# Fourier mixing and a hard-swish MLP on one core: the inverse transform's last stage as even and odd sums of mirrored tokens

## The chip, the cores and the metric

The kernel runs on one core of one Trainium2 chip. The metric is device microseconds of the whole program on that core; a verdict compares medians of several runs on the same chip. The core's engines are named as in the profile: PE (TensorE, with PEld for its weight loads), DVE (VectorE), ACT (ScalarE), POOL (GpSimd) and SP (SyncE, which here only issues DMAs).

## The reference

All data are 32-bit floats. `x` has 8 batches of 3008 tokens with 256 features.

```python
X = np.fft.rfft(x, axis=1)
Y = X * (filt_r + 1j * filt_i)[None, :, :]
y = np.fft.irfft(Y, n=3008, axis=1)
t = y.reshape(8 * 3008, 256)
h = t @ w_in                           # 256 -> 2048
g = h * np.clip(h + 3.0, 0.0, 6.0) / 6.0
out = g @ w_out                        # 2048 -> 256
```

## The kernel before

**The transform.** 3008 tokens are 47 times 64. A batch goes through four stages, each a set of small matrix products with tables of cosines and sines: `a_unit` and `b_unit` forward, a product with the filter (`f_unit`, `y_unit`, on VectorE), `bi_unit` and `n_unit` back. Between `bi_unit` and `n_unit` the values go through a tensor in DRAM: `g_store` (L497) writes it, `t4_load` (L520) reads it, because the next stage needs other rows on the partitions.

The last stage, `n_unit` (L534), makes tokens. For each of 32 values j it has 4 blocks of 24 rows (real and imaginary parts for two mirrored halves, at partitions 0, 32, 64 and 96 of the 128), which are multiplied with a table `wai` of 94 columns: 47 tokens 64 apart that start at j, and 47 that start at the mirrored place 64-j. `chunks` (L508) puts five values of j into a group: 5 matmuls of 94 columns make 470 columns in one PSUM bank, twice, once for each half of the 256 features (`dh`). So a batch has 6 groups of five and one of two; the first batch has an own opening group of six. ScalarE copies the bank (L543) into `xn`, a ring of three MLP blocks.

**The MLP.** It works in 47 blocks of 512 tokens. Block 0 is computed plainly (`plain_up`, `plain_down`). Each later block is cut into halves of 256 tokens, and both products are done with 7 multiplications of halves instead of 8 (a Strassen form). That needs sums of the weights, made once by GpSimd in `w_sums` (L304) with the lists `IN_SUMS` and `OUT_SUMS` (L319, L321), and sums of the token halves, made by GpSimd for each block in `t_sums` (L572), 4 of 128x256. `up_1` to `up_5` (L585 to L624) multiply, `hswish` and `g_sums` make the activations and their sums on VectorE, `down` (L651) multiplies back, `out_1` to `out_5` put four accumulators together in `o`, and `store` (L723) writes the 512 tokens to the output: runs of at most 47 rows of 1 KB each, since neighbouring tokens of a block lie 64 rows apart in the output. There are 14 or 15 such runs in a block.

**The order.** It is written out by hand. A step is an eighth of a block (376 steps). The two loops at the end put the MLP's instructions of a step down, and `plan` (L741) says which units of the transform go into which step, ahead of or behind the MLP's own. `t4_load` of a group is issued one step behind the second `n_unit` that last used its half of the buffer `t4`; the first group of a batch can't be loaded before the last `g_store`, so its load stands only 3 steps ahead of its units (L895). SP issues all loads and the stores, in that order and one after the other; POOL issues `z_store` and `g_store` between its sums. In the built program, each DMA issued by SP or ACT takes the next of eight semaphores in turn, and waits first until the DMA that had it before has landed.

At the end (L1000 to L1007) the last block's 14 runs are cut into pieces of a multiple of 16 rows and a rest, and spread over the queues of SP, ACT and POOL.

Of the kernel before, what the change touches and what calls it, by code (L numbers as in the profile page):

```python
# [11 lines left out]
I32 = mybir.dt.int32  # L12
# [38 lines left out]
RING = 3 * BLK  # L51
ND = (NJ + 1) * TOK


def outer(j, h):

    return (NC - j if j else HC) if h else j


def _make_tables():  # L60
# [3 lines left out]
    wai = np.zeros((P, HC, TOK))  # L64
# [26 lines left out]
    for q in range(64):  # L91
# [3 lines left out]
        wi[q, 3], wi[HALF + q, 3] = ab, sign * ab  # L95

        at = g % 2 * 32 + (q // 2 if q < 32 else 16 + (q - 32) // 2)
        wi[at, 0], wi[HALF + at, 0] = ab, sign * ab
# [11 lines left out]
        wi[q, 1], wi[HALF + q, 1] = ab, -ab  # L110
        wi[q, 2], wi[HALF + q, 2] = sign * ab, sign * ab
    start[:, :P] = np.eye(P)
    for j in range(HC):
        for h in range(2):
            to = slice(h * NA, (h + 1) * NA)
            for k in range(KH):
                m = 2.0 if k else 1.0
                th = 2 * np.pi * ((a * k * NC + outer(j, h) * k) % N) / N
                cs, sn = m * np.cos(th), m * np.sin(th)
                s = -1.0 if h else 1.0  # L120
                if j:
                    wai[k, j, to], wai[32 + k, j, to] = cs, -sn
                    wai[64 + k, j, to], wai[96 + k, j, to] = -s * sn, -s * cs
                else:
                    wai[h * 64 + k, j, to], wai[h * 64 + 32 + k, j, to] = cs, -sn
    direct = np.zeros((P, TC, ND))
    n = np.array([i * NC + outer(j, h) for j in range(NJ + 1) for h in range(2) for i in range(NA)])
    for k in range(KH - TC, KH):
        for q in range(64):
            th = 2 * np.pi * (((k + NA * q if q < 32 else NA * (q - 31) - k) * n) % N) / N  # L130
            direct[q, k - KH + TC], direct[HALF + q, k - KH + TC] = 2 / N * np.cos(th), -2 / N * np.sin(th)
    f = np.float32
    return wa.astype(f), (wai / N).astype(f), wb.astype(f), wi.astype(f), wf.astype(f), start.astype(f), direct.astype(f)
# [3 lines left out]
def kernel(  # L137
# [22 lines left out]
    g0_d = nc.dram_tensor("g0_tmp", (NC, 2, KH, D), FP32, kind="Internal").ap()  # L160
    g_d = nc.dram_tensor("g_tmp", (B, NU, 2, 2, NC, D), FP32, kind="Internal").ap()
# [22 lines left out]
    wai = const.tile([P, HC, TOK], FP32, name="wai")  # L184
# [3 lines left out]
    t4 = const.tile([P, 2 * NJ, D], FP32, name="t4")  # L188
    xn = const.tile([P, 2, RING], FP32, name="xn")
# [64 lines left out]
    def w_load(i, q):  # L254
        if W_AT[i] == "g":
            t = gp.tile([P, 7, 256], FP32, name="g")
            st["rest"] = t[:, 4:7, :].rearrange("p a n -> p (a n)")
            t = t.bitcast(I32)[:, 0:4, :].rearrange("p a n -> p (a n)")
        elif W_AT[i] == "x":
            t = xtp.tile([P, 4, 256], FP32, name="xt").bitcast(I32).rearrange("p a n -> p (a n)")  # L260
        else:
            t = op.tile([P, 1024], I32, name="bits", tag="o")
        q.dma_start(t.rearrange("p (a d) -> p a d", a=2), w_part(i)[0])
        st["bits", i] = t
# [39 lines left out]
    def w_sums(i, late):  # L304
        w = (w_in, w_out)[i % 2][i // 2]
        for o, x0, x1, op_ in (IN_SUMS, OUT_SUMS)[i % 2][3 * late:3 + late]:
            nc.gpsimd.tensor_tensor(out=w[:, o, :], in0=w[:, x0, :], in1=w[:, x1, :], op=op_)

# [9 lines left out]
    A11, S3, A12, A22, S1, S2, S4 = range(7)  # L318
    IN_SUMS = ((4, 1, 3, ALU.add), (5, 4, 0, ALU.subtract), (6, 2, 5, ALU.subtract), (1, 0, 1, ALU.subtract))  # L319
# [27 lines left out]
    def zt(dh):  # L347
        return (xn.rearrange("p a n -> p (a n)"), xs.rearrange("p i j d -> p (i j d)"))[dh]
# [141 lines left out]
    def g0_first(i):  # L490
        t = st["t3", 0, i]
        for v in range(2):
            for h in range(2):
                (nc.scalar, nc.sync)[v].dma_start(g0_d[ds(h * HC, NJ + 1), :, ds(2 * (i + v), 2), :].rearrange("c ri u d -> c ri (u d)"),
                                    t[ds(v * 64 + h * HC, NJ + 1)].rearrange("p ri u d -> p ri (u d)"))

    def g_store(b, i):  # L497
        t = st.pop(("t3", b, i))
        for v in range(2):
            if b == 0:  # L500
                nc.gpsimd.dma_start(g0_d[:, :, ds(2 * (i + v), 2), :].rearrange("c ri u d -> c ri (u d)"),
                                    t[ts(v, 64)].rearrange("p ri u d -> p ri (u d)"))
                continue
            nc.gpsimd.dma_start(g_d[b, i + v].rearrange("ri u c d -> c (ri u) d"), t[ts(v, 64)].rearrange("p ri u d -> p (ri u) d"))  # L504
# [4 lines left out]
    for b in range(B):  # L509
        j = 0  # L510
        while j < HC:
            n = 1 if b == 0 and j == NJ else min(NJ, HC - j)
            chunks.append((b, j, n))
            j += n

    def token(i):
        b, j, n = chunks[i]
        return b * N + j * TOK, n * TOK

    def t4_load(i, k0=0, k1=KH, more=0):  # L520
        b, j, n = chunks[i]
        n += more
        for h in range(2):
            for ri in range(2):
                p0 = h * 64 + ri * 32
                if b == 0:
                    nc.sync.dma_start(t4[p0 + k0:p0 + k1, ds(i % 2 * NJ, n), :],
                                      g0_d[ds(h * HC + j, n), ri, k0:k1, :].rearrange("j k d -> k j d"))
                    continue
                nc.sync.dma_start(t4[p0 + k0:p0 + k1, ds(i % 2 * NJ, n), :].rearrange("k j d -> k (j d)"),  # L530
                                  g_d[b, k0 // 2:k1 // 2, ri, :, ds(h * HC + j, n), :].rearrange("i u j d -> i u (j d)"))


    def n_unit(i, dh):  # L534
        ps = psF.tile([P, 512], FP32, name="psn", tag="f")
        for q in range(chunks[i][2]):
            nc.tensor.matmul(ps[:, ts(q, TOK)], t4[:, i % 2 * NJ + q, ts(dh, P)], wai[:, chunks[i][1] + q, :], start=True, stop=True)  # L537
        t, n = token(i)
        done = 0
        while done < n:  # L540
            o = (t + done) % RING
            m = min(n - done, RING - o)
            nc.scalar.activation(out=xn[:, dh, ds(o, m)], in_=ps[:, ds(done, m)], func=AXT.Copy)  # L543
            done += m
        if dh and (t + n) // BLK > t // BLK > 0:
            t_sums(t // BLK)


    def direct(i):
# [4 lines left out]
        for u in range(2):  # L554
            k = 2 * i + u - KH + TC
            for (c, dh), ps in st["psn"].items():
                t, n = token(c)
# [3 lines left out]
    def n_first():  # L561
        for (c, dh), ps in st.pop("psn").items():
            b, j, n = chunks[c]
            for q in range(n):
                nc.tensor.matmul(ps[:, ts(q, TOK)], t4[:, j + q, ts(dh, P)], wai[:, j + q, :],
                                 start=False, stop=True, skip_group_check=True)
            nc.scalar.activation(out=xn[:, dh, ds(j * TOK, n * TOK)], in_=ps[:, 0:n * TOK], func=AXT.Copy)

    def xb(k, d):
        return xn[:, d, ts(k % 3, BLK)]  # L570

    def t_sums(k):  # L572
        t = xtp.tile([P, 4, 256], FP32, name="xt")
        b11, b12, b21, b22 = (xb(k, d)[:, ts(h, 256)] for d in range(2) for h in range(2))
        for o, x0, x1 in ((0, b12, b11), (1, b22, t[:, 0, :]), (2, b22, b12), (3, b21, t[:, 1, :])):
            nc.gpsimd.tensor_tensor(out=t[:, o, :], in0=x0, in1=x1, op=ALU.subtract)
        st["xt", k] = t

# [4 lines left out]
    def up_1(k, p):  # L585
# [5 lines left out]
        product(al, p, A11, xb(k, 0)[:, 0:256], start=True)  # L591
        product(be[:, 1, :], p, S1, t[:, 0, :], start=True)
        product(be[:, 0, :], p, A12, xb(k, 1)[:, 0:256])
# [4 lines left out]
    def up_2(k, p):  # L598
# [3 lines left out]
        product(al, p, S2, t[:, 1, :])  # L602
        product(be[:, 1, :], p, S4, xb(k, 1)[:, 256:512], stop=True)
# [7 lines left out]
    def up_3(k, p):  # L611
        al, be, s, s5 = st["up"]
        product(al, p, S3, st["xt", k][:, 2, :])
# [6 lines left out]
    def up_5(k, p):  # L620
        al = st["up"][0]
        product(al, p, A22, st["xt", k][:, 3, :], stop=True)
# [42 lines left out]
    def plain_up(p):  # L665
        st["g", 0, p] = gp.tile([P, 7, 256], FP32, name="g")
        st["h"] = [psU.tile([P, 512], FP32, name=n) for n in ("al", "be")]
        for i in range(2):
            for d in range(2):
                nc.tensor.matmul(st["h"][i], w_in[p][:, 2 * d + i, :], xb(0, d), start=d == 0, stop=d == 1)  # L670
# [14 lines left out]
    def plain_out():  # L685
# [4 lines left out]
        store(0, 0, 4)  # L690
# [26 lines left out]
    def out_5(k):  # L717
        nc.vector.tensor_tensor(out=o_at(k, 0, 1), in0=st.pop(("po", k))[3][:, 1, :, :], in1=o_at(k, 0, 1), op=ALU.add)
        store(k, 0, 4)
# [3 lines left out]
    def store(k, u0, u1, qs=None):  # L723
        o = st["o", k][0].rearrange("p t u d -> p (t u) d")
        t, end, i = k * BLK + u0 * P, k * BLK + u1 * P, 0
        while t < end:
            b, r = divmod(t, N)
            j, r = divmod(r, TOK)
            h, a = divmod(r, NA)
            p = t % P  # L730
            m = min(NA - a, P - p)
            if qs:
                m = m // 16 * 16 or m
            q = qs[i % len(qs)] if qs else nc.sync
            i += 1
            q.dma_start(raw(out, b * N + a * NC + outer(j, h), [[NC * D, m], [1, D]]),  # L736
                              o[p:p + m, t % BLK // P, :])
            t += m
# [10 lines left out]
    with tc.manual_schedule():  # L749
# [67 lines left out]
        nc.sync.dma_start(wai[:, 0:8, :], wai_d[:, 0:8, :])  # L817
        load_bits(4)
        turn(0)
        for c in range(NT):  # L820
# [10 lines left out]
            if c == 4:  # L831
                t4_load(0, 0, KH - 3 * TC, 1)
        t4_load(0, KH - 3 * TC, KH - TC, 1)
# [18 lines left out]
        def wai_load():  # L852
            nc.sync.dma_start(wa[:, 528:], wa_d[:, 528:])
            nc.sync.dma_start(wai[:, 8:HC, :], wai_d[:, 8:HC, :])
# [27 lines left out]
        for i in range(2, len(chunks)):  # L882
            in_block.setdefault(token(i)[0] // BLK, []).append(i)
        stored = 0
        for i in range(2, len(chunks)):
            k = token(i)[0] // BLK
            head = chunks[i][1] == 0
# [116 lines left out]
        store(k, 2, 4, qs)  # L1004
        v(out=o_at(k, 0, 1), in0=po[2][:, 0, :, :], in1=o_at(k, 0, 1), op=add)
        v(out=o_at(k, 0, 1), in0=po[3][:, 1, :, :], in1=o_at(k, 0, 1), op=add)
        store(k, 0, 2, qs)  # L1007
# [30 lines left out]
```

## Time and profile before

| | us |
|---|---|
| time before, median of 3 runs | 2697.59 (2697.15 to 2698.23) |
| span of the profiled execution, first to last instruction | 2694.8 |
| the median less that span | 2.8 |
| PE busy, of the span | 2674.4 (99%) |
| DVE busy | 2021.7 (75%) |
| ACT busy | 1305.4 (48%) |
| POOL busy | 368.4 (14%) |

The page states the span of the execution that it profiles and not its time; the 2.8 us are what the runs' median has beyond that span.

In the page's second part, which cuts the span into 40 slices, PE has the digit 9 in 39 slices and 8 in the last, and the clock granted to it is 9 tenths or more throughout. The DMA engines' share is 8 tenths in the first slice and 1 to 3 in most others. The page's fifth part puts the records into groups by line: a line of it gives the engine, the operation, the tiles and their shapes, the count, the busy time, the mean duration in ns, and how long the engine was idle just ahead of these, with what ended that idle time. A matmul of the program stands in the trace as two records, so the 500 matmuls of `n_unit` are 1000 records of L537. The duration of a PE record overlaps that of the next; how fast PE goes is read from the distance between starts.

### The profile page before, as it was taken

The numbers are of one execution on the slowest core, as the hardware profiler recorded it, in microseconds if no ns is written. First come the engines' busy times: TensorE is split into PE (matmuls) and PEld (weight loads), VectorE is DVE, ScalarE is ACT, GpSimd is POOL, SyncE is SP. The second block draws the span as 40 slices with busy tenths as digits, with TensorE's granted clock in tenths as the row PEclk, the third lists the DMA queues.
The fourth block names the chain that finished last, engine by engine and source line by source line (L and its number), as shares of the span: only waits on it lengthen the run. The fifth ranks groups of instructions, "written<-read, shape, count | busy, mean of one in ns | idle before, by whom it ended". The sixth has DMA issues, their size and how long they took to land.

```text
span 2694.8 us, 48891 instructions
## 1 busy us (share of the span) xinstructions
PE 2674.4 (99%) x18846; PEld 2366.1 (88%) x18846; DVE 2021.7 (75%) x3505; ACT 1305.4 (48%) x2612; POOL 368.4 (14%) x598
## 2 busy tenths in 40 slices
PE   9999999999999999999999999999999999999998
PEld 6688898888888888888898888888888888899997
DVE  7978867877678776787767877677876878766665
ACT  3444444444445454454544544545444454445443
POOL 2141021001210112101121111211012111000000
PEclk9999999999999999999999999999999999999999
DMA  8732133211331113311133112331123321110000
GB/s 239 220 96 65 48 97 97 63 36 49 91 101 55 37 52 92 96 55 38 51 92 96 55 40 54 88 95 55 40 56 91 91 61 33 42 31 18 18 9 17
DMA packets 106598, 185.89 MB, mean 69 GB/s; under 512 B 23609, under 2 KB 66297, under 8 KB 106049
## 3 DMA queue, kind: packets, MB, share of 16 engines
q1 hardware_dynamic: 88607, 138.05, 18.1%
q0 software_dynamic: 17152, 44.22, 6.2%
q8 instruction: 149, 2.44, 0.4%
q14 instruction: 84, 0.69, 0.1%
q10 hardware_dynamic: 606, 0.49, 0.1%
HBM read 110.74 MB, written 71.93 MB: 68 GB/s over the span
## 4 chain that ended last, share of the span: by engine, by line
PE 98%; DVE 1%; issue 0%; ACT 0%; POOL 0%; DMA 0%; POOLq 0%; SPq 0%; DVEq 0%
PE po L659 43%; PE al L583 24%; PE be L583 18%; PE psn L537 4%; PE psf L393 2%; PE psf L484 2%; PE psf L440 1%; PE po L681 1%; PE po L360 1%; PE al L670 0%; PE be L670 0%; PE psf L449 0%; PE po L449 0%; PE al L796 0%; POOL out_dram L736 0%
## 5 line engine op out<-in xcount | busy, mean ns | idle before, releaser
L659 PEld LDWEIGHTS po<-w_all,g 128*128 128x128 f32 x10304 | 1363.4, 191 | 149.2 <-issue 41.4
L659 PE MATMUL po<-w_all,g 128*128 128x128 f32 x10304 | 1403.1, 276 | 0.6 <-DVE g L633 0.6
L628 ACT ACTIVATE r<-h,half_c 128x512 f32<-128x512 f32 x736 | 531.1, 722 | 329.2 <-DVE h L609 317.1
L633 DVE SCALAR_TENSOR_TENSOR g<-r,h 128x512 f32<-128x512 f32 x736 | 507.8, 690 | 205.0 <-ACT r L628 191.0
L583 PE MATMUL al<-xt,w_all 128*128 128x256 f32 x2208 | 660.0, 381 | 0.7 <-DVE h L614 0.6
L583 PE MATMUL be<-xn,w_all 128*128 128x256 f32 x1472 | 437.8, 379 | 0.0
L609 DVE TENSOR_TENSOR h<-be,s 128x512 f32<-128x512 f32 x368 | 254.1, 691 | 215.7 <-PE be L583 210.7
L583 PEld LDWEIGHTS al<-xt,w_all 128*128 128x128 f32 x2208 | 335.3, 192 | 2.1 <-DVE h L614 1.2
L583 PEld LDWEIGHTS be<-xn,w_all 128*128 128x128 f32 x1472 | 279.7, 190 | 37.9
L623 ACT ACTIVATE h<-al 128x256 f32<-128x256 f32 x368 | 141.0, 383 | 344.1 <-PE al L583 344.1
L614 DVE TENSOR_TENSOR h<-al,s 128x256 f32<-128x256 f32 x368 | 156.0, 424 | 166.0 <-PE al L583 165.0
L641 DVE TENSOR_TENSOR g<-g 128x512 f32<-128x512 f32 x368 | 256.2, 696 | 12.7
L604 ACT ACTIVATE s<-al 128x256 f32<-128x256 f32 x368 | 141.2, 384 | 206.2 <-PE al L583 204.1
L595 ACT ACTIVATE s<-be 128x256 f32<-128x256 f32 x368 | 141.0, 383 | 176.7 <-PE be L583 176.7
L583 PE MATMUL al<-xn,w_all 128*128 128x256 f32 x736 | 219.9, 381 | 0.5 <-ACT h L623 0.5
L583 PE MATMUL be<-xt,w_all 128*128 128x256 f32 x736 | 218.9, 379 | 0.0
L643 DVE TENSOR_TENSOR g<-g 128x256 f32<-128x256 f32 x368 | 170.1, 462 | 12.5
L594 ACT ACTIVATE s<-al 128x256 f32<-128x256 f32 x368 | 141.0, 383 | 70.8 <-PE al L583 70.8
L640 DVE TENSOR_TENSOR g<-g 128x256 f32<-128x256 f32 x368 | 157.3, 427 | 12.6
L583 PEld LDWEIGHTS be<-xt,w_all 128*128 128x128 f32 x736 | 139.8, 190 | 18.9
L414 POOL DMA_DIRECT2D z_tmp<-t x192 | 95.2, 502 | 417.6 <-DVE t L407 399.3
L504 POOL DMA_DIRECT2D g_tmp<-t x84 | 52.7, 632 | 582.1 <-ACT t L487 582.1
(144 smaller groups left out, 1816.0 us busy)
## 6 DMA issues: line engine op xcount, KB each, us to landing
g_tmp<-t POOLq DMA_DIRECT2D x96, 256.0 KB, 3.7
t<-g_tmp SPq DMA_DIRECT2D x188, 120.0 KB
t<-z_tmp SPq DMA_DIRECT2D x42, 512.0 KB
z_tmp<-t POOLq DMA_DIRECT2D x192, 96.0 KB, 3.4
out_dram<-o SPq DMA_DIRECT2D x321, 47.0 KB
xs<-in_x_dram SPq DMA_DIRECT2D x112, 128.0 KB
ft<-in_filt_r_dram SPq DMA_DIRECT2D x168, 64.0 KB
ft<-in_filt_i_dram SPq DMA_DIRECT2D x168, 64.0 KB
```

The lines of the kernel that those rows point to most:

```text
L583: nc.tensor.matmul(ps, w_in[p][:, w, :], x, start=start, stop=stop, skip_group_check=True)
L594: nc.scalar.activation(out=s[:, 0, :], in_=al, func=AXT.Copy)
L595: nc.scalar.activation(out=s5, in_=be[:, 1, :], func=AXT.Copy)
L604: nc.scalar.activation(out=s[:, 1, :], in_=al, func=AXT.Copy)
L609: nc.vector.tensor_tensor(out=st["h"][0].rearrange("p (a n) -> p a n", a=2), in0=be, in1=s, op=ALU.add)
L614: nc.vector.tensor_tensor(out=st["h"][1][:, 256:512], in0=al, in1=s5, op=ALU.add)
L628: nc.scalar.activation(out=r, in_=st["h"][i], func=AXT.Relu, bias=half_c, scale=1.0 / 6.0)
L633: nc.vector.scalar_tensor_tensor(out=st["g", k, p][:, o:o + 2, :].rearrange("p a n -> p (a n)"), in0=st["r", i], scalar=1.0, in1=st["h"][i ...
L640: v.tensor_tensor(out=g[:, G1, :], in0=g[:, G3, :], in1=g[:, G22, :], op=ALU.add)
L641: v.tensor_tensor(out=g[:, G3:G2 + 1:2, :], in0=g[:, G3:G1 + 1, :], in1=g[:, G11:G11 + 1, :].broadcast_to([P, 2, 256]), op=ALU.subtract)
L643: v.tensor_tensor(out=g[:, G4, :], in0=g[:, G12, :], in1=g[:, G2, :], op=ALU.subtract)
L659: nc.tensor.matmul(st["po", k][bank][:, part, u, :], g[:, a, ts(u, P)], w_out[p][:, w, :], start=(p == 0 and n in OPENS and u == 0), stop= ...
```

## The change

The last stage doesn't make tokens any more but, for each pair of mirrored tokens, an even sum C and an odd sum S, with the tokens C-S and C+S. C needs only 48 of the 96 rows (24 of each mirrored half), S the other 48. Five j have 240 such rows, which are packed without gaps into two weight loads of 128 and 112 rows, one pair of loads for C and one for S; each is multiplied with 141 columns of a table (three times 47), and the two results overlap in 47 columns, where they add up in PSUM. The values j = 0, 1 (and 6 in the first batch) have matmuls of their own with 96 rows and 94 columns.

The MLP's halves of a block are now the two members of 256 pairs. `xn` holds C and S, not tokens; the subtraction and addition that would make the tokens are folded into `t_sums` (7 sums instead of 4) and into the weights' sums (two of the seven are multiplied by 2 and -2, on ScalarE).

The second half of a block's output now belongs to tokens in mirrored order. It is stored whole to a tensor in DRAM, `o_tmp`, and from there copied, DRAM to DRAM, to its places, each row in two pieces of 512 bytes. Only the first half goes straight to the output.

```diff
-            n = 1 if b == 0 and j == NJ else min(NJ, HC - j)
-            chunks.append((b, j, n))
+        js = list(range(2 if b else NJ + 2, HC))
+        parts = [js[i:i + NJ] for i in range(0, len(js), NJ)]
+        parts = parts + [[0, 1]] if b else [list(range(NJ)), [NJ]] + parts + [[NJ + 1]]
...
     def t4_load(i):
-                nc.sync.dma_start(t4[p0 + k0:p0 + k1, ds(i % 2 * NJ, n), :].rearrange("k j d -> k (j d)"),
-                                  g_d[b, k0 // 2:k1 // 2, ri, :, ds(h * HC + j, n), :].rearrange("i u j d -> i u (j d)"))
+        for q, j in enumerate(js):
+            for hh in range(2):
+                r, k = q * ATOM + hh * KH, 0
+                while k < KH:
+                    s_, p0 = divmod(r + k, P)
+                    m = min(KH - k, P - p0)
+                    nc.sync.dma_start(both[p0:p0 + m, s_, :, :],
+                                      g_d[b, hh * HC + j, :, k:k + m, :].rearrange("ri k d -> k ri d"))
+                    k += m
...
     def n_unit(i, dh):
-        for q in range(chunks[i][2]):
-            nc.tensor.matmul(ps[:, ts(q, TOK)], t4[:, i % 2 * NJ + q, ts(dh, P)], wai[:, chunks[i][1] + q, :], start=True, stop=True)
+            for c in range(2):
+                for s_ in range(2):
+                    r = ROWS[s_]
+                    nc.tensor.matmul(ps[:, ds(c * NJ * NA + s_ * 2 * NA, SPAN)], t4[0:r, s0 + 2 * c + s_, ts(dh, P)],
+                                     groups[0:r, (js[0] - 2) // NJ, s_, :], start=c == 0 and s_ == 0, stop=True,
+                                     skip_group_check=True)
...
     def t_sums(k):
-        for o, x0, x1 in ((0, b12, b11), (1, b22, t[:, 0, :]), (2, b22, b12), (3, b21, t[:, 1, :])):
-            nc.gpsimd.tensor_tensor(out=t[:, o, :], in0=x0, in1=x1, op=ALU.subtract)
+        for o, x0, x1, op_ in ((f1, c0, s0, ALU.subtract), (u, c0, c1, ALU.add), (v, s0, s1, ALU.add),
+                               (f4, u, v, ALU.subtract), (f5, u, v, ALU.add), (f2, c1, s1, ALU.add), (f3, f1, f2, ALU.add)):
+            nc.gpsimd.tensor_tensor(out=o, in0=x0, in1=x1, op=op_)
...
     def w_sums(i, late):
+        if late and i % 2 == 0:
+            for o, scale in ((S1, 2.0), (A22, -2.0)):
+                nc.scalar.activation(out=w[:, o, :], in_=w[:, o, :], func=AXT.Copy, scale=scale)
...
     def out_5(k):
-        store(k, 0, 4)
+        store(k, 1)
+        store(k, 0)
+        store_back(k)
...
+    def store(k, h, q=nc.sync):
+        o = st["o", k][0]
+        if h:
+            nc.sync.dma_start(o_d[k % 2].rearrange("u p d -> p u d"), o[:, h, :, :])
+            return
+        for u, p, m, b_, j, a in runs(k):
+            q.dma_start(raw(out, b_ * N + row(j, 0, a), [[NC * D, m], [1, D]]), o[p:p + m, 0, u, :])
...
+    def store_back(k, q=nc.sync):
+        src, half = o_d[k % 2], D // 2
+        for u, p, m, b_, j, a in runs(k):
...
+            q.dma_start(bass.AP(tensor=out.tensor, offset=out.offset + (b_ * N + min(ends)) * D,
+                                ap=[[half, 2], [NC * D, m], [1, half]]),
+                        bass.AP(tensor=src.tensor, offset=src.offset + r0 * D, ap=[[half, 2], [step, m], [1, half]]))
...
         v(out=o_at(k, 1, 0), in0=st["o", k][1][:, 1, :, :], in1=o_at(k, 1, 0), op=add)
-        store(k, 2, 4, qs)
+        store(k, 1)
         v(out=o_at(k, 0, 1), in0=po[2][:, 0, :, :], in1=o_at(k, 0, 1), op=add)
         v(out=o_at(k, 0, 1), in0=po[3][:, 1, :, :], in1=o_at(k, 0, 1), op=add)
-        store(k, 0, 2, qs)
+        store(k, 0, nc.scalar)
+        store_back(k)
```

`runs` yields the pieces of at most 47 rows in which a block's 256 pairs lie (7 or 8 a block). `g_store` writes the tensor that `t4_load` reads in one layout for all batches, with 2 KB pieces in place of 1 KB ones. The products of `up_1` to `up_5` are as many and as large as before; five of the seven now read a sum of `t_sums` and two read `xn`. `wai` is loaded whole in step 0, over the opening group's part of it.

## The prediction

> **What bounds the kernel now.** I read the page's busy table first, then its chain of waits, then the timeline of TensorE.
>
> ```profile
> span 2694.8 us, 48891 instructions
> PE 2674.4 (99%) x18846; PEld 2366.1 (88%) x18846; DVE 2021.7 (75%) x3505; ACT 1305.4 (48%) x2612; POOL 368.4 (14%) x598
> ...
> PE 98%; DVE 1%; issue 0%; ACT 0%; POOL 0%; DMA 0%; POOLq 0%; SPq 0%; DVEq 0%
> ```
>
> TensorE is never without work and is 98% of the chain: whatever it issues less is time. The rest of the chain is the opening and the end. The profiled execution's span is 2694.8 us; the median run, 2697.59, is 2.8 above it, which I take to lie around the span and to stay. All sums start from 2694.8.
>
> **The removed TensorE work.** How far apart do records start? Each matmul of the program makes two.
>
> ```profile
> 1002.62 0.59 PE L583 MATMUL be<-xt,w_all 128*128 128x256 f32 x2
> 1003.05 0.59 PE L583 MATMUL be<-xn,w_all 128*128 128x256 f32 x2
> ...
> 11.66 3.74 PE L360 MATMUL po<-p,w_all 111*128 111x128 f32 x32
> 15.23 1.02 PE L796 MATMUL al<-r 128*128 128x512 f32 x2
> ...
> 1024.21 2.20 PE psn L537 x20
> ```
>
> 256 columns: 0.43 for two, so 215 ns each. 128 columns: (15.23-11.66)/32 = 112. And the last stage's 94 columns: 2.20/20 = 110, no cheaper than 128. The step from 112 to 215 over 128 columns is 0.81 ns a column, so 94 columns should take 84; something the size of a 128-column weight load holds them at 110. That is what the change attacks. Five j now take 4 matmuls (8 records) of 141 columns instead of 5 (10 records) of 94. 141 columns are past the floor: 112 + 13x0.81 = 122 by these rows, 118 by the slope of the 512-column row (1.72 us for four records, 430 each); I take 120. A unit goes from 1.09 to 0.96. There are 94 full units (6x2 in each of 7 batches, 5x2 in the first): 94x0.13 = **-12 us** (-10 to -13). The 2-wide and 1-wide units keep their matmul counts. The new loads have 128, 112 or 96 rows; the L360 row has 111 and follows and precedes 128-row work at its ordinary spacing, so I charge nothing for mixing.
>
> **What goes beside TensorE.** (a) t_sums: 7 GpSimd sums a block instead of 4, 46x3 more at 0.73 (L576's rows show 742 and 747 ns) = 100 us on an engine that is 14% busy. After the second half of the feature columns arrives, 6 sums remain instead of 3, 2.2 us more. The tightest blocks (n_unit at steps 6,6) have their last sum end 9 us ahead of the block's first product (1029.0 against 1038.5 in GpSimd's and TensorE's timelines), so nothing waits; if that cover were gone it would cost at most 2.2x46 = 100. VectorE pays a little beside GpSimd: L643 (SBUF alone) averages 462 ns where L614, the same size, takes 424; 38 ns over 368 is 14 us of slowed VectorE now, some 10 more then, on an engine that is 75% busy. I charge **+1** (0 to +5). (b) n_unit's copy keeps 470 elements, only its output is in two strips; the pair [0,1] takes two copies instead of one on an engine at 48%: 0. (c) g_store writes the same bytes in longer pieces: 0.
>
> (d) The 16 ScalarE scalings wait for GpSimd's weight sums, and everything behind them on ScalarE waits too.
>
> ```profile
> 125.65 25.17 POOL L307 TENSOR_TENSOR w_all<-w_all 128x128 f32<-128x128 f32 x43 [20.39 <-DMA z_tmp<-t]
> ...
> 128.94 0.69 ACT L269 ACTIVATE s<-bits 128x512 f32<-128x512 f32 x1
> 132.04 0.38 ACT L594 ACTIVATE s<-al 128x256 f32<-128x256 f32 x1 [2.41 <-PE al L583]
> ```
>
> The sums start at 125.65 and go at 0.585 each. The first pair of scalings needs the sixth (129.2), the second pair the fourteenth (133.8). ScalarE reaches them at 121.5 and some 132; relu of plain step 7 moves from 125.2 to 129.5, which plain_down hides, and L594 of the next step from 132.0 to 134.1, when TensorE at 133.82 needs it: 0.7 late. In step 11, 7 sums stand ahead of the weights': 0.4 late. The first t4 loads (22 transfers instead of 8) push the raw weights' loads 4 to 5 us back, mostly beside conversions that are paced by VectorE. I take **+1.5** (0 to +6).
>
> **SP's queue.** The listing of the built program shows eight DMA semaphores taken in turn by what SP and ACT issue: each transfer waits for the landing of the eighth before it. A group is 11 transfers instead of 4, and each block's 15 stores become one store to o_tmp, 7 or 8 stores and as many copies back.
>
> ```profile
> 993.59 14.03 SPq L736 DMA_DIRECT2D out_dram<-o  x15
> 1007.66 1.72 SPq L330 DMA_DIRECT2D xs<-in_x_dram  x4
> 1009.75 5.71 SPq L530 DMA_DIRECT2D t<-g_tmp  x4
> ...
> 2649.61 1.93 SPq L736 DMA_DIRECT2D out_dram<-o  x1
> ```
>
> A store of 47 rows in a backlog holds SP for 1.93 us, 41 ns a row. A half row (512 bytes, DRAM to DRAM) is in no row here: by bytes 20 ns, by count 41, twice that if reading and writing add. I take 30. Seven batches begin with a load that must be in before n_unit (1024.05 here). After the change: 993.6 + 1.2 for the first store, 195 rows at one pace x41 = 8.0, 256 half rows x30 = 7.7, landing 2.4 (the stores' rows show 2.0 to 2.7): 1012.9; seven more issues at 0.45 and a landing: 1018.5, 5.5 us early. So 0, up to 52 ns a half row. Other groups' loads come 30 us or more ahead.
>
> **The end.** This decides.
>
> ```profile
> 2685.23 4.71 SPq L736 DMA_DIRECT2D out_dram<-o  x10
> 2685.23 3.68 ACTq L736 DMA_DIRECT2D out_dram<-o  x8
> 2685.57 0.42 DVE L1006 TENSOR_TENSOR o<-po,o 128x256 f32<-128x256 f32 x1
> ```
>
> VectorE ends at 2685.99 = t. Now three queues issue short pieces for 4 us and the span ends at t+8.8: 4.0 issue, 2.4 landing, 2.4 closing. In the changed listing the semaphores are not in SP's order: block 45's third copy back waits for a semaphore that block 46's first ACT store has to raise, and ACT issues that store only after t. So SP stands from about 2643 on; behind it are only the rest of block 45's copies and block 46's stores, and no load, so nobody but the end waits. After t: ACT's six stores up to the one that frees SP's store to o_tmp, 154 to 209 rows at 41 = 7.3, +0.5 +2.4; block 45's five copies (167 half rows) between them, +2; block 46's store to o_tmp, issued only now, 3.7 (the page's g_tmp store of that size); seven copies back, 256 half rows x30 = 7.7, +0.5 +2.4; closing 2.4. (A copy is written as two columns of half rows; I let the columns run side by side, each at the pace of a 47-row store, its nearest row. One behind the other they take 15.4; spread over all engines only their issue counts, 3.2.) Sum t+28.9, against t+8.8: **+20**. Low end: 6.3 of rows, no copies between, 2.4 for o_tmp, copies at 3.2: +10. High end: 8.6 of rows, 6.8, 3.7, copies at 15.4, landings 2.7: +34.
>
> A rule bears on these copies: by the Trainium skill, "DMA: Bandwidth & Descriptors", section "Why a DMA increments its semaphore by 16 and not by 1", a DMA is split over the largest number of engines up to 16 that divides its slowest dimension, the lowest-numbered ones. The 1.93 us of 47 rows agrees (one engine). It speaks against this change: a copy back with outer dimension 2 would use two engines, one of them the stores' own. By the rule an estimate of the copies is the 7.7 above; were they spread like 128-row transfers they would be hidden in their issue, 3.2, and the end +15.
>
> **Sum:** 2694.8 -12 +1 +1.5 +20 = 2705.3, +2.8 = **2708**. Ends: -13 and +10 give 2695; -10 +5 +6 +34 give 2733.
>
> **Rivals.** (1) Faster: the stall at the end does not bite, because ACT's stores and the copies land beside each other in their issue time. Place: t to the end. Under +4 there, the sum is below -5.4 and faster; at +3, 2691. For it: the engines' share is 0.19 after 2685 in the windows view. Against it: the semaphore order is in the program, and 47-row stores take 1.93 each. (2) Within 0.2% (2692.2 to 2703.0, about what a measurement tells from no change): TensorE's gain and an end of +4 to +14, the low end of the working; 2699. (3) Slow half rows: at 82 ns the loads of seven batches come 256x30 = 7.7 late (54 in all) and the end is 13 longer: 2775; at 60, 2731. For it: nothing here goes DRAM to DRAM; against it: 1 KB rows go at 41.
>
> **Chances.** Forecast 0.62 (own range 2703 to 2722), rival 1 0.08, rival 2 0.20, rival 3 0.10. Slower 0.62+0.10 = 0.72, same 0.20, faster 0.08. The range leaves out rival 1 and the worse part of rival 3: 2695 to 2733.
>
> **What would show it.** Right: L537's successor has 8 records a unit, 120 ns apart; VectorE's last add about 10 us earlier than 2685.57, and the span's end some 29 us after it, with SP's copies of two blocks in between. Wrong: n_unit waiting for a DMA at batch heads (rival 3), gaps on ACT beyond 2 us in 125 to 165, or an end under 15 us.

## The result and the profile after

The changed kernel takes 2707.15 us (median of 5 runs, 2706.35 to 2707.99) against 2697.59 of the kernel before on the same chip: ratio 1.0036, 95% interval 1.0025 to 1.0047. Slower by 9.6 us, where 10.4 were forecast. The profiled execution has a span of 2704.5.

The busy table and the first line of the chain of waits, after:

```profile
span 2704.5 us, 49025 instructions
...
PE 2664.2 (99%) x18658; PEld 2352.2 (87%) x18658; DVE 2072.4 (77%) x3505; ACT 1310.1 (48%) x2644; POOL 492.0 (18%) x728
...
PE 93%; DVE 4%; DMA 1%; SPq 1%; issue 0%; ACT 0%; POOL 0%; DVEq 0%; ACTq 0%; POOLq 0%
```

TensorE has 188 records and 10 us of busy time less, and yet the span is longer: the 10 us went where TensorE is not busy. VectorE is busy 51 us more, GpSimd 124. A unit of five j, both halves, in the chain of waits (start, length, engine, tile, line, records):

```profile
1024.66 1.93 PE psn L603 x16
```

and the records of the same line (count, shortest/median/longest ns, first and last start, shape):

```profile
L603 PE MATMUL psn<-wai,t x752: 281/283/286, 90.9 to 2549.2; 128*128 128x141 f32 x188
```

16 records of 141 columns in 1.93, so 120.6 ns each, where 20 of 94 columns took 2.20. The end, from the timelines of VectorE, ACT and SP (start, time from the first issue to the last):

```profile
2677.76 0.42 DVE L1105 TENSOR_TENSOR o<-po,o 128x256 f32<-128x256 f32 x1
2678.22 3.97 ACTq L816 DMA_DIRECT2D out_dram<-o  x7
2643.89 0.59 SPq L835 DMA_DIRECT2D out_dram<-o_tmp  x1
2679.66 8.77 SPq L835 DMA_DIRECT2D out_dram<-o_tmp  x5
2689.17 0.67 SPq L813 DMA_DIRECT2D o_tmp<-o  x1
2694.64 4.54 SPq L835 DMA_DIRECT2D out_dram<-o_tmp  x7
```

VectorE ends at t = 2678.2, 7.8 earlier than before; the span ends at t+26.3 instead of t+8.8. The fourth line is SP's last issue before it stands; the next is 35.8 us later. Then come the five copies of block 45 that stood in its queue, then block 46's store to o_tmp at t+11, then, when that has landed, its copies.

**Step by step.** Comparing the starts of the same step (its first up_1 record) in the two traces gives the account: how much later or earlier the changed kernel is.

| start of step | before, us | after less before |
|---|---|---|
| 8 | 131.41 | +0.84 |
| 9 | 140.17 | +2.36 |
| 12 | 164.40 | +1.74 |
| 13 | 171.41 | +2.84 |
| 32 | 313.35 | +3.10 |
| 136 | 1038.50 | +0.16 |
| 200 | 1484.05 | -1.95 |
| 375, the last | 2673.19 | -7.50 |

Each unit is worth 149 ns; from step 8 on the steps that gain, gain 12.6 in all. 4.2 are lost again: 1.52 in step 8, 1.10 in step 12, 0.35 and 0.37 in steps 28 and 44, and 0.1 to 0.15 in each of seven others, which I did not follow up. Ahead of step 8, 0.8 are lost: step 7 starts 0.06 later than before, and the product that opens step 8 starts 0.84 later. This is step 7's loss in what follows. Of what came earlier, some 0.4 are the opening's, which waits for the loads of x and comes a few tenths to 1 us earlier or later from run to run of either kernel; two units have gained 0.1 each and a little. From the start of the last step to t another 0.3 are gained. So -7.8 to t and +17.5 behind it make the +9.7 of the spans.

### The profile page after: what moved, and what is told of

It reads as the page before. It is cut to its first block, busy times and chain, and to the rows that moved or that the text cites. A ratio compares the mean times of both kernels' runs of the same rounds, so it can differ in the third digit from the quotient of the medians.

```text
span 2704.5 us, 49025 instructions
## 1 busy us (share of the span) xinstructions
PE 2664.2 (99%) x18658; PEld 2352.2 (87%) x18658; DVE 2072.4 (77%) x3505; ACT 1310.1 (48%) x2644; POOL 492.0 (18%) x728
## 4 chain that ended last, share of the span: by engine, by line
PE 93%; DVE 4%; DMA 1%; SPq 1%; issue 0%; ACT 0%; POOL 0%; DVEq 0%; ACTq 0%; POOLq 0%
PE po L742 42%; PE al L666 23%; PE be L666 17%; PE psn L603 3%; PE psf L524 2%; PE psf L433 2%; PE psf L480 1%; DVE g L716 1%; PE po L400 1%; PE po L489 0%; DVE y L317 0%; DVE w_all L338 0%; DVE y L335 0%; DVE y L333 0%; PE psf L489 0%
## 5 line engine op out<-in xcount | busy, mean ns | idle before, releaser
L711 ACT ACTIVATE r<-h,half_c 128x512 f32<-128x512 f32 x736 | 531.0, 721 | 342.8 <-DVE h L692 330.8
L716 DVE SCALAR_TENSOR_TENSOR g<-r,h 128x512 f32<-128x512 f32 x736 | 531.3, 722 | 199.0 <-ACT r L711 185.3
L666 PE MATMUL be<-xt,w_all 128*128 128x256 f32 x1472 | 437.8, 379 | 0.0
L666 PEld LDWEIGHTS be<-xt,w_all 128*128 128x128 f32 x1472 | 279.7, 190 | 37.9
L662 POOL TENSOR_TENSOR xt<-xn 128x256 f32<-128x256 f32 x184 | 154.5, 852 | 660.9 <-ACT xn L618 632.4
L666 PE MATMUL be<-xn,w_all 128*128 128x256 f32 x736 | 219.0, 379 | 0.0
L726 DVE TENSOR_TENSOR g<-g 128x256 f32<-128x256 f32 x368 | 177.2, 481 | 12.5
L677 ACT ACTIVATE s<-al 128x256 f32<-128x256 f32 x368 | 141.2, 384 | 67.2 <-PE al L666 67.2
L723 DVE TENSOR_TENSOR g<-g 128x256 f32<-128x256 f32 x368 | 157.7, 429 | 12.6
L666 PEld LDWEIGHTS be<-xn,w_all 128*128 128x128 f32 x736 | 139.8, 190 | 19.1 <-DVE g L716 0.2
```

The source lines that it names most:

```text
L662: nc.gpsimd.tensor_tensor(out=o, in0=x0, in1=x1, op=op_)
L666: nc.tensor.matmul(ps, w_in[p][:, w, :], x, start=start, stop=stop, skip_group_check=True)
L711: nc.scalar.activation(out=r, in_=st["h"][i], func=AXT.Relu, bias=half_c, scale=1.0 / 6.0)
L716: nc.vector.scalar_tensor_tensor(out=st["g", k, p][:, o:o + 2, :].rearrange("p a n -> p (a n)"), in0=st["r", i], scalar=1.0, in1=st["h"][i ...
L723: v.tensor_tensor(out=g[:, G1, :], in0=g[:, G3, :], in1=g[:, G22, :], op=ALU.add)
L726: v.tensor_tensor(out=g[:, G4, :], in0=g[:, G12, :], in1=g[:, G2, :], op=ALU.subtract)
```

## The experiments

**The detour and the end.** My theory was that the loss is the end's; the rivals, that it lies in the steps, or that the copies cost something all along. Four kernels ran beside the kernel before (2697.31).

First, the last block's first half stored by SP:

```diff
-        store(k, 0, nc.scalar)
+        store(k, 0)
         store_back(k)
```

> The changed kernel with one word different: the last block's seven stores of its first half go on SP, behind its store to o_tmp, instead of on ACT. SP's DMAs then take their semaphores in SP's own order, and nothing of block 45 waits for block 46. Theory (SP stands behind ACT's stores, and everything of block 46's second half is issued only after them): VectorE ends where it did, 2678.2 (t); SP issues the store to o_tmp during the last adds, the seven stores until t+4, the seven copies 4.5 more as in the changed run, and landing and closing take the 5.3 that they took there: t+14, span 2692, time about 2695, 12 below the changed kernel and 0.999 of the kernel before. Rival (the standing costs nothing by itself; 47-row stores and copies at 1.9 each set the end wherever they are issued): the end stays above t+22, time 2703 or more. Rival (the loss lies in the steps, not at the end): time within 2 of the changed kernel's 2707.

Measured: 2699.45, ratio 1.0008 (0.9999 to 1.0016).

```profile
2678.72 0.42 DVE L1105 TENSOR_TENSOR o<-po,o 128x256 f32<-128x256 f32 x1
2679.17 4.14 SPq L816 DMA_DIRECT2D out_dram<-o  x7
2683.36 9.26 SPq L835 DMA_DIRECT2D out_dram<-o_tmp  x7
```

In these lines of the timelines SP stands no more, and the end is t+18.9 (span 2698.0). The size was wrong, though: the copies behind the seven stores take 9.3 to issue, not 4.5. So the standing is not the whole price, and something in the copies and stores themselves costs as much again.

Second, no detour at all:

```diff
-        if h:
-            nc.sync.dma_start(o_d[k % 2].rearrange("u p d -> p u d"), o[:, h, :, :])
-            return
+                at_ = min(row(j, h, a), row(j, h, a + n - 1))
+                (qs[i % 3] if k == NBLK - 1 else q).dma_start(raw(out, b_ * N + at_, [[NC * D, n], [1, D]]), o[p:p + n, h, u, :])
...
-        store_back(k)
```

> The changed kernel without the detour: the second halves go straight from o to the output, in rising order (so the rows of each run are put down the wrong way round; that order is what this kernel leaves out), with as many stores as the kernel before has; the last block's in pieces of a multiple of 16 rows on three queues, as before. Theory (end 17.5, and a stall of 1.1 in step 12 where SP brings z_store and the first t2 load late): the end comes back to t+9, and step 12 waits no more: span 2677+9 = 2686, time 2689, ratio to before 0.997. Rival (the copies also cost TensorE or VectorE time all along, by the DRAM traffic that they add): VectorE's last add comes well ahead of 2677, time under 2685. Rival (most of the loss is elsewhere): over 2695.

Measured: 2691.95, ratio 0.9978 (0.9969 to 0.9987); VectorE ends at 2679.83, the span at 2688.7, t+8.9. Without the detour the change is faster than the kernel before. VectorE does not end earlier than with the detour (2678.2) but 1.6 later, 1.05 of it in step 12, and from step 13 on the starts of the steps move as in the changed kernel. So the 46 other blocks' copies cost nothing that shows: that rival falls. My own addition about step 12 falls too: its stall grew to 2.15, since 14 stores now held SP as long as seven stores and seven copies had.

**GpSimd's sums.** The kernel before, with three sums made twice:

```diff
+        for o, x0, x1 in ((1, b22, t[:, 0, :]), (2, b22, b12), (3, b21, t[:, 1, :])):
+            nc.gpsimd.tensor_tensor(out=t[:, o, :], in0=x0, in1=x1, op=ALU.subtract)
```

> The kernel before with three of t_sums' four GpSimd sums made a second time, so seven a block, with the same values. The prediction charged the three more sums +1 (0 to +5), by what VectorE pays beside GpSimd. The changed kernel shows three small losses (0.35, 0.37, 0.15) where VectorE instructions beside GpSimd take 1.11 us in place of 0.70. Theory: VectorE's busy time rises by some 40 us, the time by 1: 2698.6. Rival (this contention is where most of the 4 us went that the changed kernel lost against the forecast of its steps): +4, 2701.6. Rival (the cover is gone and products wait for the sums): +20 or more.

Measured: 2697.86, ratio 1.0004 (0.9995 to 1.0013). VectorE's busy time rises to 2060.7, by 39.0, and the steps lose 0.36 in step 26 and 0.35 in step 28 and nothing from there on: +0.7. VectorE pays much, the time little: VectorE is still idle for 24% of the span.

**The floor.** The kernel before, with 47 columns a matmul:

```diff
+            for h in range(2):
+                nc.tensor.matmul(ps[:, ds(q * TOK + h * NA, NA)], t4[:, i % 2 * NJ + q, ts(dh, P)], wai[:, chunks[i][1] + q, ts(h, NA)],
+                                 start=True, stop=True)
```

> The kernel before with each 94-column matmul of n_unit cut in two of 47 columns, each with its own weight load; 500 matmuls become 1000, and 1000 records 2000. Theory of the floor (94 columns are held at 110 ns a record by something that does not fall with the columns, as the prediction read it): 47-column records also stand 110 apart, 1000 x 0.11 = +110, time 2808. Rival (the time of a record falls with its columns, by 0.81 ns a column: 94 columns cost 84 and the rest is a start of the unit): 47 columns stand 46 to 60 apart, time within 15 of before.

Measured: 2818.43, ratio 1.0449 (1.0430 to 1.0468).

```profile
1069.63 4.40 PE psn L538 x40
```

40 records in 4.40: 110 ns each with 47 columns, as with 94. The rival falls. What holds the records there stays argued: the prediction took it to be the load of the weights, which have 128 columns in every one of these matmuls, and no run changed that number. The units alone account for 112 of the 121 us (1.117 for each of 94, the pairs' units the rest); the other 9 lie in a few steps with two units, and I did not trace them.

**The losses of steps 7, 8 and 12.** Where do they come from? The waits view of the changed kernel between 126 and 146 us (who waited for whom: us in total, times, longest) has three waits of TensorE that the kernel before does not have:

```profile
PE al L666 <- DVE g L716: 0.6, 1, 0.6
PE al L666 <- ACT s L677: 0.6, 1, 0.6
...
PE po L764 <- DVE w_all L338: 0.4, 1, 0.4
```

Then ACT in the timeline; the bracket has its idle time ahead of the instruction and what ended that:

```profile
129.42 0.31 ACT L347 ACTIVATE w_all<-w_all 128x128 f32<-128x128 f32 x1 [7.86 <-POOL w_all L344]
...
130.71 0.67 ACT L711 ACTIVATE r<-al,half_c 128x512 f32<-128x512 f32 x1
```

ACT stands 7.9 us at the first scaling, and relu (L711) behind it runs at 130.7, which was at 125.2 before. All three waits follow from that. up_1's first product of step 8 writes the PSUM tile `al`, which `hswish` of plain step 7 must read first; behind the late relu that is done at 132.1, and the product starts at 132.25: step 7's 0.8. ACT's copy L677 stands behind the second pair of scalings and ends at 135.5: 0.65 in step 8. VectorE stood 4.1 us for relu, so its next weight conversion (L338) ends at 137.7, and `plain_down` waits for it: another 0.5. The rest of step 8's 1.5 is in pieces of 0.2 and less. A11, the sum that up_1's first product needs, is ready at 130.9 and holds nothing here. In step 12 TensorE waits for a transfer:

```profile
PE psf L489 <- DMA t<-z_tmp: 0.6, 1, 0.6
```

Two kernels took one suspect away each; a third took both away and mended the end as well. The late copy:

```diff
-        store_back(0)
+        at(16, store_back, 0)
```

> The changed kernel with block 0's seven copies back issued in step 16 instead of right behind its stores in step 8. In the changed kernel TensorE loses 1.1 us in step 12 against the kernel before (2.2 where the copies were replaced by seven more stores): b_unit waits for the first t2 load of batch 1, which stands on SP behind z_store, block 0's stores and copies, and the first t4 loads of 11 transfers. Theory (SP's queue): with the copies' 7.9 us gone from there, z_store and the t2 load come 7 earlier and step 12's loss is 0; time 1 below the changed kernel, 2706. Rival (the t2 load is late because a_unit's results are, which the queue doesn't change): the loss of 1.1 stays.

Measured: 2707.13, ratio 1.0036 (1.0023 to 1.0049); step 12's loss is 1.11, as before. But the wait is another one. The t2 load is issued 5.1 earlier (159.20 against 164.33), and TensorE now waits for ACT's copy L677, which stands behind the scalings of its step (168.31 and 169.77):

```profile
PE al L666 <- ACT s L677: 0.8, 1, 0.8
```

The late scaling:

```diff
-        if late and i % 2 == 0:
-            for o, scale in ((S1, 2.0), (A22, -2.0)):
-                nc.scalar.activation(out=w[:, o, :], in_=w[:, o, :], func=AXT.Copy, scale=scale)
...
+                if i % 2 == 0:
+                    at(7 + i // 2, w_scale, i)
```

> The changed kernel with the 16 ScalarE scalings of the weights' sums issued one step later than the sums, ahead of that step's other work, instead of right behind them. In the changed kernel ScalarE stands 12 us for GpSimd's sums (7.9 at once), and TensorE loses 0.8 us in step 7 and 1.5 in step 8 against the kernel before. Theory (the scalings hold up relu and the copies queued behind them): both losses fall below 0.3 each; time about 2 below the changed kernel, 2705. Rival (GpSimd's sums themselves come 1.8 us later, because conversions do, and products wait for those): the losses stay within 0.5 of what they were.

Measured: 2706.95, ratio 1.0035 (1.0022 to 1.0049). Step 7 loses 0.65, step 8 still 1.7, step 12 1.3. The waits of step 8 (the same view) and of step 12:

```profile
PE al L667 <- ACT s L688: 1.6, 1, 1.6
PE psf L490 <- DMA t<-z_tmp: 1.1, 1, 1.1
```

So step 12 has two holds of the same length side by side, the load and the scalings, and each covers the other. Neither theory's number came out, and only the kernel with both edits (below) shows that both were real: its step 12 loses nothing. In step 8 the rival's number came out, but the wait shows another reason than the rival's. The late scalings free relu; but the next part's two scalings now stand in step 8 ahead of ACT's copy L688, and wait for GpSimd until 137.29, so the copy is late and TensorE waits 1.6 for it. In step 7 up_1's first product now waits for A11 itself, as the rival had it: the sum ends at 133.11, the product starts at 133.16. Late sums by themselves cost nothing: in the kernel before with seven sums a block, which has no scalings and no sum in that product, GpSimd's weight sums also start at 127.3, and steps 7 and 8 lose nothing. What costs is what the change makes wait for them, ScalarE above all. So the next test makes the sums early:

```diff
-        order = [2 * NP - 3] + [i for i in range(2 * NP) if i != 2 * NP - 3]
-        for i in order:
...
+        for i in range(2 * NP):
+            at(6 + i // 2, w_sums, i, False)
+            at(6 + i // 2, w_sums, i, True)
+            if i % 2 == 0:
+                at(7 + i // 2, w_scale, i)
```

> The version with all three mends, and GpSimd's weight sums in their natural order: in both kernels the sums of part 13 stand first and wait on GpSimd for a conversion that VectorE ends only at 127.3, so all other sums wait too. In the changed kernel up_1's first product needs the fourth and last sum of its part (the new A11), where before it needed none; late scalings did not change step 8's loss of 1.5 to 1.7 us. Theory (that product and the scalings wait for GpSimd's sums, which start too late): with part 13 in its own turn the sums start some 5 us earlier and step 8's loss falls below 0.4; time 1.3 below the version without this edit, 2687.7, ratio to before 0.9964. Rival (ScalarE's copies are late for another reason): the loss of 1.5 stays.

Measured: 2690.21, ratio 0.9974 (0.9963 to 0.9984). The sums start at 109.6 instead of 128.2 (the version without this edit), no scaling waits for them any more (130.99 and 137.58 in ACT's timeline), and step 8 loses 0.03. Its later start by 2.9 would alone cover its 1.7; that the scalings no longer wait is what shows the cause. Yet the time is no better than the version without this edit (2688.97, ratio 0.9968): step 8 now starts 4.4 after the kernel before, where that version's starts 1.5 after, and only 0.6 of these 2.9 are the opening's. TensorE's waits ahead of step 8 grow where VectorE is full of conversions beside GpSimd:

```profile
PE al L754 <- DVE g L717: 2.9, 3, 1.3
```

Without the edit that line reads 1.3. The gain was given back in another place.

**The end, taken apart.** Two suspects: SP stands (stores on ACT) or doesn't (stores on another queue), and the copies' rows go in two pieces or in 16. Three more kernels complete the four combinations; where both are mended, the copies also go on two queues (SP and ACT). Other queue and 16 pieces:

```diff
-        store(k, 0, nc.scalar)
-        store_back(k)
+        store(k, 0, nc.gpsimd)
+        store_back(k, (nc.sync, nc.scalar), 16)
...
-                                ap=[[half, 2], [NC * D, m], [1, half]]),
+                                ap=[[half, cut], [NC * D, m], [1, half]]),
```

> The changed kernel with another end: the last block's seven stores of its first half go on GpSimd's queue, whose semaphores are its own, and its seven copies back go on SP and ACT in turn, each row in 16 pieces of 64 bytes with the piece as the outer dimension, instead of two of 512. With the stores on SP the end was t+18.9 instead of t+26.3 (t is VectorE's end), of which the copies took 9.3 behind the stores. Theory (the copies are held by the one or two engines that they and the stores share): o_tmp lands by t+4.5, four copies a queue take 2, landing and closing 5.4: t+12, span 2690.5, time 2693.5, ratio to before 0.9985. Rival (what takes time is the chain of two landings, store and copy, whoever issues): t+16 or more, time over 2697. Rival (64-byte pieces are dearer than they look): over t+20.

Measured: 2690.69, ratio 0.9974 (0.9964 to 0.9985).

```profile
2678.35 0.42 DVE L1105 TENSOR_TENSOR o<-po,o 128x256 f32<-128x256 f32 x1
2679.06 3.58 POOL L816 DMA_DIRECT2D out_dram<-o  x7 [45.56 <-DVE o L1105]
2680.17 2.66 SPq L835 DMA_DIRECT2D out_dram<-o_tmp  x4
2680.18 2.26 ACTq L835 DMA_DIRECT2D out_dram<-o_tmp  x3
```

The store to o_tmp lands by t+1.4 and the copies are issued by t+4.0: the whole end is t+9.2, 2.8 better than expected and 0.4 longer than the 8.8 of the kernel before.

16 pieces alone:

```diff
-        store_back(k)
+        store_back(k, cut=16)
```

> The changed kernel with the last block's copies back cut in 16 pieces of 64 bytes a row (the piece the outer dimension) in place of two of 512; the stores stay on ACT, so SP stands as before. Taken with the end on other queues, this completes the four combinations: SP standing or not, two pieces or 16. Theory (the two costs are separate: standing 7 to 11, copies 3 or more): SP still issues the store to o_tmp at t+11 and it lands at t+16; the copies then take their issue, 3.2, and 3.5 for landing and closing: t+23 against t+26.3, time 2704. Rival (the cut is what counts): under t+16, time below 2697.

Measured: 2705.53, ratio 1.0032 (1.0020 to 1.0044); end t+24.6 (2683.38 to 2708.0). In this execution the clock granted to TensorE was 0.97 up to 131 us and t 5 us late; the end is read from t, which that doesn't touch.

The other queue alone:

```diff
-        store(k, 0, nc.scalar)
+        store(k, 0, nc.gpsimd)
         store_back(k)
```

> The changed kernel with the last block's first-half stores on GpSimd's queue, so that SP doesn't stand and its copies have SP for themselves, in two pieces of 512 bytes a row as in the changed kernel. Theory (512 pieces of 27 ns on two engines take 6.9, however free the queue is): store to o_tmp landed at t+2, copies 7 to 9, landing and closing 3.5: t+13 to t+15, time 2695. Rival (once SP doesn't stand, the copies hide in their issue of 3.2 and the cut into 16 added nothing): t+9 to t+10, time 2691, as with 16 pieces. Rival (copies and stores share engines as they did with the stores on SP): t+18, time 2699.

Measured: 2693.06, ratio 0.9984 (0.9975 to 0.9993).

```profile
2678.41 0.42 DVE L1105 TENSOR_TENSOR o<-po,o 128x256 f32<-128x256 f32 x1
...
2680.24 5.53 SPq L835 DMA_DIRECT2D out_dram<-o_tmp  x7
```

| end, counted from t | two pieces | 16 pieces |
|---|---|---|
| SP stands (stores on ACT) | 26.3 | 24.6 |
| SP stores and copies | 18.9 | not run |
| stores on GpSimd's queue | 12.4 | 9.2 (copies on SP and ACT) |

The standing is 13.9 to 15.4 of the 17.5, the cut 1.7 to 3.2; the larger number of each pair has the second queue for the copies in it. The first run's 18.9 lies between. Its packets show the stores' 1 KB rows still being moved until 2690.2, 6.9 us into the issue of the copies, which fits stores of 47 rows that hold up the copies behind them; no run separates the two.

**All mends together:**

> The three edits together: late copies of block 0, late scalings, and the end on three queues with 16 pieces a row. If the losses are separate, the gains add: 1.1 in step 12, 2 in steps 7 and 8, 14 at the end. Theory: time 2690.5, ratio to before 0.9975 (0.997 to 0.998), faster than both kernels. Rival (a mended stall only lets the next one through): above 2693.

Measured: 2688.97, ratio 0.9968 (0.9955 to 0.9980), faster than both kernels; end t+9.1, step 12's loss 0, step 8's 1.7 as with the late scaling alone. That is 1.5 better than expected.

## Why the prediction was right, and where only its sum was

**TensorE, -12: right, a little small.** 94 columns are at a floor, as read from the 112 ns of 128 columns; 47 columns show it outright. The gain of a unit is 149 ns instead of 130. The sum left out the four records of `down` behind it, which take 0.44 instead of 0.48. Behind each of the 64 units that stand alone that is some 30 of the 149; where two units stand together it comes once for both, 15 each, beside 135 by their own records. Mixed loads of 128 and 112 rows cost nothing that shows: 120.6 a record, where 118 to 122 were worked out. A rule of the Trainium skill bears on this, "TensorE: Matmul & The Clock Gate", section "LDWEIGHTS (loading the stationary operand)": a weight load takes its number of columns divided by 1.2, in ns, whatever the rows. For 128 columns that is 107, an estimate by the page's formula; the runs show records 110 apart.

**GpSimd's sums, hidden and +1: right in price, wrong in size.** VectorE was slowed by 39 us (run with doubled sums), not by some 10. Only two places pay, 0.7 together. In the steady state the tightest block's last sum ends at 1032.0, 6.6 ahead of the product, close to the 7.3 worked out. What I missed is the setup. Beside the new sums VectorE's weight conversions at 104 to 109 us take up to 1.10 instead of 0.69 (VectorE's timeline, the changed kernel; L338 and L315 are 0.69 and 0.42 where GpSimd is idle):

```profile
105.62 1.09 DVE L335 SCALAR_TENSOR_TENSOR y<-y 128x512 f32<-128x512 f32 x1
106.75 1.10 DVE L338 SCALAR_TENSOR_TENSOR w_all<-s,y 128x512 f32<-128x512 f32 x1
107.77 0.95 DVE L315 TENSOR_SCALAR y<-bits 128x512 int32<-128x512 int32 x1
```

Conversions run without a gap there, so the lost time stays lost, and GpSimd's weight sums start 1.8 later, at 127.45. The kernel before with seven sums shows the same (127.34).

**The scalings and first loads, +1.5: mis-sized, 3.4 measured** (0.8 in step 7, 1.5 in step 8, 1.1 in step 12). The way of the loss was right: scalings wait for GpSimd's sums, and what is behind them on ScalarE waits too. The step that failed is "relu of plain step 7 moves from 125.2 to 129.5, which plain_down hides": it moved to 130.7, and up_1's first product, which needs what `hswish` makes free behind relu, waited 0.8. In step 8 the 0.7 charged for the copy behind the second pair of scalings came out (0.65); the 0.5 of the weight conversion, which VectorE put off while it stood for relu, were not in the sum. Step 12 was half seen: the sum had 0.4 for scalings there (in step 11, as it counted), and for SP's queue it had checked only t4 loads, not batch 1's t2 load behind two groups of 11 transfers and block 0's copies.

**SP's queue, 0: right at the batch heads.** Around the one that I worked out, after:

```profile
994.04 7.28 SPq L816 DMA_DIRECT2D out_dram<-o  x8
1001.36 9.31 SPq L835 DMA_DIRECT2D out_dram<-o_tmp  x8
1010.71 1.75 SPq L370 DMA_DIRECT2D xs<-in_x_dram  x4
1012.84 4.49 SPq L588 DMA_DIRECT2D t<-g_tmp  x11
```

The load starts at 1012.84 (1012.9 in my sum) and its last transfer is issued at 1017.3; with a landing of 2 to 2.7 that is about 5 ahead of n_unit at 1024.66. A half row takes 27 ns in the trace's packets (30 taken), so the third rival was far off. What the queue did delay, besides the end, is the t2 load of step 12 above.

**The end, +20: the mechanism right, +17.5 measured, its parts of other sizes.** In the trace's semaphores block 45's five copies take, one after the other, those of ACT's first five stores, and block 46's store to o_tmp that of the sixth, as the prediction had it. SP's waits view shows four of these copies, and the store to o_tmp, waiting for the landing of such a store. The copies are issued from t+1.5 on (the first three at 2679.66, 2682.84, 2685.70), the store to o_tmp at t+11 (t+12.2 in my sum). That store takes 5.5 (3.7). The copies take 4.5 to issue and 5.3 from there to the end of the span (landing and closing), 9.8 instead of 13.0. The four combinations show the standing to be the larger part by far, where the sum had charged the standing some 12 of its 20.

A second rule stood behind the copies, "DMA: Bandwidth & Descriptors", section "Why a DMA increments its semaphore by 16 and not by 1": with 2 as the outer dimension, two engines. In the packets of the changed kernel the last block's 512 half rows of 27 ns take 6.8 us: 2.0 engines busy on average; beside the stores on SP they take 9.9 us, 1.4 engines. With 16 as the outer dimension, 4096 pieces of 64 bytes at some 11 ns take 3.1 us on two queues and 4.8 on one: some 15 and 9 engines. These stay within the rule's two and sixteen; no view shows which engine moved a packet.

**The total** agreed to 0.8 us of span because errors cancelled: t came 1.7 later than in the sum (-7.8 for -9.5), the end 2.5 earlier.

## What to carry to other kernels

Read the end as a stage of its own: a DMA there that waits for another queue's work, through a semaphore that both take in turn, costs more than all the work that was saved; put stores that depend on the last result on a queue whose semaphores no one else needs. When a stall has two holds of equal length, removing one shows nothing; test both together before dropping either. And an engine with idle time on average can be full in the setup: what is added beside it is priced there. On an engine that takes its work in order, an instruction that waits for another engine holds all behind it; moved a step later it held the next copy, and only earlier input took the wait away.

## What the runs showed of the hardware that I had not expected

- A DRAM-to-DRAM row in 16 pieces of 64 bytes as the outer dimension is quicker than in two of 512: dearer by the byte (11 ns for 64 against 27 for 512), but the end is 1.7 shorter on the same queue, and 3.2 in the run whose copies also had two queues instead of one.
- A matmul record at the floor is not quite free of its columns: the four 128-column records behind a unit take 0.44 after 141 columns, 0.48 after 94, 0.53 after 47.
- VectorE instructions beside GpSimd's sums are stretched from 0.42 to 0.95 and from 0.69 to 1.10, whole instructions at a time; on average over the run this is 39 us of VectorE for 130 of GpSimd.
